# ScalarE writes the high halves of the projection phase, and two first-segment transposes use the score banks

## The chip, the cores and the metric

The kernel runs on one core of one Trainium2 chip. The metric is the device time of one execution in microseconds, median of the runs; lower is better.

## The reference

One transformer block over 2048 tokens of width 576, in fp32: adaptive layer norm, attention with 32 heads of width 18 in four segments of 512 tokens with a compressive memory carried from segment to segment, a residual, a second adaptive layer norm, a gated feed-forward layer of width 4608, and a second residual. Cut to what matters:

```python
mod = (silu(c) @ w_mod).reshape(1, 6, 1, 576)        # sa, ca, ga, sb, cb, gb
h = layernorm(x) * (1 + ca) + sa
q, k, v = h @ wq, h @ wk, h @ wv                      # 32 heads of 18, 4 segments of 512
for s in range(4):
    p = softmax(q_s @ k_s.T * scale + causal_mask)
    a_dot = p @ v_s
    a_mem = (phi(q_s) @ M) / (phi(q_s) @ z + 1e-6)    # phi(t) = t + 1 if t > 0 else exp(t)
    o_s = g * a_mem + (1 - g) * a_dot
    M, z = M + phi(k_s).T @ v_s, z + phi(k_s).sum()
x = x + ga * (concat(o) @ wo)
h = layernorm(x) * (1 + cb) + sb
x = x + gb * ((silu(h @ w_gate) * (h @ w_up)) @ w_down)
```

## The kernel before

Matrix products are made in a reduced fp32 format (F32R). To keep fp32 accuracy, an operand is split into a high part `hi` (the value rounded to F32R) and a low part `lo = x - hi`, and a product is made of three terms: high by high, low by high, high by low. Making a high part is one pass of an engine over the tile; making a low part is a subtraction on VectorE.

The kernel is one program without loops at run time. Python writes the instructions, and a planner then fixes the order of each engine's instructions from the order they were written in and from estimated durations; on the chip each engine works through its own list strictly in that order. The lists can therefore differ from the written order.

Three stages follow each other: the projection phase (the function's first part, pools opened at lines 244 to 251), the attention phase with the output projection, and the feed-forward layer. The change is in the projection phase only.

**Start.** TensorE multiplies the modulation weights `wm` with the conditioning vector into `pr` (line 356). ScalarE copies `pr` to `row` (lines 360 and 363), TensorE transposes it (`pcr`, line 367), and VectorE writes the per-feature scale and shift `colv` (lines 370 to 372). In the meantime VectorE normalises the first segment's four tiles of `x` in place (line 229).

**Transposed activations, `trans_in(s)`, line 408.** For each of five feature tiles `kt`, TensorE transposes the normalised `x` into a PSUM tile `pt` of tag `t`, which has two banks (line 234). `evac_split` (line 236) follows: ScalarE applies scale and shift from PSUM to an SBUF tile `f` (line 241, tag `hf`, two buffers), and `split` (line 78) makes the high part on GpSimd from `f` (line 79) and the low part on VectorE (line 80). The results are `hh[kt]` and `hl[kt]`, and for the last, half-filled tile `hr`, which holds both parts. They have one buffer each, so a segment's tiles can be written only when the value projection of the segment before has read the old ones.

**Query and key projection, `proj(s, t)`, line 456.** For each of nine output tiles, 14 matrix products accumulate in a bank `pp` (tag `p`, three banks; line 99). The bank is read once: ScalarE copies it to `f` (line 464), GpSimd makes `fh` from `f`, VectorE makes `fl`, and the queue of SyncE stores both to memory (lines 469 to 478). For key tiles `phi_k` (line 431) transposes `f` (`ptk`, line 435) and makes the feature map.

**Weights.** `split` is also used for the nine weight tiles `wqkh`/`wqkl` (line 294) and the five tiles `wvh`/`wvl` (line 511), each after its load (`wraw`, `wvraw`; four buffers).

**Other work of the phase.** `vproj` (line 483) makes the values (`pv`) and copies them out on ScalarE (line 496). `mem` (line 442) makes the memory matrices (`pm`), with a VectorE product (line 451) and a GpSimd sum (line 453). From segment 1 on, `early` begins the scores of the first two attention units: products in banks of tag `s1` (line 182), maxima on VectorE (line 187), a small GpSimd step (`mc`, `ml`, lines 192 to 195), a transpose `pmt` (line 201). The statistics of the next segment's layer norm use VectorE and one GpSimd power (`rs`, line 225). The eight PSUM banks are: two of tag `t`, three of `p`, one of `m`, two of `s1`.

Of the kernel before, what the change touches and what calls it, by code (L numbers as in the profile page):

```python
# [7 lines left out]
F32 = mybir.dt.float32  # L8
F32R = mybir.dt.float32r
BF16 = mybir.dt.bfloat16  # L10
AF = mybir.ActivationFunctionType
ALU = mybir.AluOpType
# [3 lines left out]
P = 128  # L16
# [6 lines left out]
L = 512  # L23
# [44 lines left out]
def f32(ap):  # L68
    return ap.bitcast(F32)
# [3 lines left out]
def block(ctx: ExitStack, tc: tile.TileContext, x, wqk, wv, wo, beta, wgu, wd, c, w_mod, out):  # L73
    nc = tc.nc
    def pool(stk, name, bufs=1, **kw):
        return stk.enter_context(tc.tile_pool(name=name, bufs=bufs, reuse_waits="tile", **kw))

    def split(hi, lo, src):
        nc.gpsimd.tensor_scalar(hi, src, 1.0, 0.0, op0=ALU.mult, op1=ALU.add)
        nc.vector.tensor_tensor(lo, src, f32(hi), op=ALU.subtract)  # L80

    def chain(*g):
# [133 lines left out]
    def ln_stats(wk, xs, n):  # L216
        st = wk.tile([P, n, 2, 6], F32, tag=f"st{n}", name="st")
        mv = wk.tile([P, n, 2], F32, tag=f"mv{n}", name="mv")
        rs = wk.tile([P, n], F32, tag=f"rs{n}", name="rs")
        for i in range(n):  # L220
            for h in range(2):
                nc.vector.bn_stats(st[:, i, h, :], xs[i][:, 288 * h:288 * h + 288])
            nc.vector.bn_aggr(mv[:, i, :], st[:, i, :, :])
        nc.vector.tensor_scalar(rs, mv[:, :, 1], EPS, None, op0=ALU.add)
        nc.gpsimd.tensor_tensor(rs, rs, mhalf[:, :n], op=ALU.pow)
        return mv, rs

    def xhat(dst, src, mv, rs, i):
        nc.vector.tensor_scalar(dst, src, mv[:, i, 0:1], rs[:, i:i + 1], op0=ALU.subtract, op1=ALU.mult)

    def transpose_group(pt, src, kt):
        for i in range(4):
            n = P if kt < 4 else 64
            nc.tensor.transpose(pt[:n, 128 * i:128 * i + 128], src(i)[:, 128 * kt:128 * kt + n], ident)

    def evac_split(wk, pt, kt, hi, lo, sc, bi, tag="hf"):
        f = wk.tile([P, L], F32, tag=tag, name="hf")
        n = P if kt < 4 else 64
        if kt == 4:
            hi, lo = hi[0:64], hi[64:128]  # L240
        nc.scalar.activation(f[:n], pt[:n], AF.Identity, scale=sc[:n], bias=bi[:n])
        split(hi, lo, f[:n])

    with ExitStack() as p1:
        wq1 = pool(p1, "wq1")
# [5 lines left out]
        ps = pool(p1, "ps1", 2, space=PSUM)  # L251
# [26 lines left out]
        def load_x(s):  # L278
            t = xs[s] = x1.tile([P, 4, D], F32, tag="x", name=f"x{s}")
            for i in range(4):  # L280
                r = L * s + P * i
                nc.sync.dma_start(t[:, i, :], x[r:r + P, :])
                yield
# [39 lines left out]
        with ExitStack() as p0:  # L323
            m0 = pool(p0, "m0")
            wm = {}
            gx = load_x(0)
            for p in (1, 0):
                for k in range(3):
                    wm[p, k] = m0.tile([96, 2, D], F32, tag=f"wm{p}{k}", name=f"wm{p}{k}")
                    nc.sync.dma_start(wm[p, k], wmv[p][:, 2 * k:2 * k + 2, :])  # L330
                    for _ in range(XP[3 * (1 - p) + k]):
                        next(gx)

            nc.scalar.activation(sg, cs, AF.Exp, scale=-1.0)
            nc.vector.tensor_scalar(sg, sg, 1.0, None, op0=ALU.add)
            nc.vector.reciprocal(sg, sg)
            nc.vector.tensor_tensor(sg, sg, cs, op=ALU.mult)

            nc.scalar.activation(gat, gat, AF.Exp, scale=-1.0)
            nc.vector.tensor_scalar(gat, gat, 1.0, None, op0=ALU.add)  # L340
            nc.vector.reciprocal(gat, gat)
            nc.vector.tensor_scalar(omg, gat, -1.0, 1.0, op0=ALU.mult, op1=ALU.add)

            for i in range(4):
                mv, rs = ln_stats(wk, [xs[0][:, i, :]], 1)
                xhat(xs[0][:, i, :], xs[0][:, i, :], mv, rs, 0)

            sgb = wk.tile([96, 6, 32], F32, tag="sgb", name="sgb", bufs=1)
            nc.vector.tensor_copy(sgb, sg.unsqueeze(2).to_broadcast([96, 6, 32]))
            pr = ps.tile([P, L], F32, tag="m", name="pr", bufs=1)  # L350
            for p in (1, 0):
                for k in range(6):
                    for h in range(2):
                        r = 64 * (1 - p) + 32 * h
                        w = wm[p, k // 2][:, k % 2, 256:576] if h else wm[p, k // 2][:, k % 2, 0:256]
                        nc.tensor.matmul(pr[r:r + 32, :320 if h else 256], lhsT=sgb[:, k, :], rhs=w,
                                         start=(k == 0), stop=(k == 5))
            row = wk.tile([P, L], F32, tag="hf", name="row")[:, :320]
            nc.gpsimd.memset(row[:, 256:], 0.0)
            nc.scalar.copy(row[:, :256], pr[:, :256])  # L360
            for p in (1, 0):
                r = 64 * (1 - p) + 32
                nc.scalar.copy(row[r:r + 32, 256:], pr[r:r + 32, 256:320])
            pc = ps.tile([P, 3, P], F32, tag="m", name="pcr", bufs=1)
            for b in range(3):
                n = P if b < 2 else 64
                nc.tensor.transpose(pc[:n, b, :], row[:, 128 * b:128 * b + n], ident)
            for p in (1, 0):
                c0 = 64 * (1 - p)
                nc.vector.tensor_scalar(colv[:, 0:2, 1 - p], pc[:, 0:2, c0], float(p), None, op0=ALU.add)  # L370
                nc.vector.tensor_scalar(colv[:, 2:4, 1 - p], pc[:, 0:2, c0 + 32], float(p), None, op0=ALU.add)
                nc.vector.tensor_scalar(colv[0:64, 4:5, 1 - p], pc[0:64, 2, c0 + 32:c0 + 33], float(p), None, op0=ALU.add)
# [35 lines left out]
        def trans_in(s):  # L408
            hh = [h1.tile([P, L], F32R, tag=f"hh{k}", name=f"hh{k}") for k in range(4)]
            hl = [h1.tile([P, L], F32R, tag=f"hl{k}", name=f"hl{k}") for k in range(4)]  # L410
            hr = h1.tile([P, L], F32R, tag="hr", name="hr")
            hT[s] = (hh, hl, hr)
            for kt in range(5):
                pt = ps.tile([P, L], F32, tag="t", name="pt")
                transpose_group(pt, lambda i: xs[s][:, i, :], kt)
                if kt < 4:
                    evac_split(wk, pt, kt, hh[kt], hl[kt], colv[:, kt, 0:1], colv[:, kt, 1:2])
                else:
                    evac_split(wk, pt, kt, hr, None, colv[:, kt, 0:1], colv[:, kt, 1:2])
                yield  # L420
# [35 lines left out]
        def proj(s, t):  # L456
            hh, hl, hr = hT[s]
            pp = ps.tile([P, L], F32, tag="p", name="pp", bufs=3)
            mm14(pp, lambda k: wqkh[:, t, k, :], lambda k: wqkl[:, t, k, :], lambda k: hh[k],
                 lambda k: hl[k], lambda: hr, True)  # L460
            f = pb.tile([P, L], F32, tag="pf", name="pf")
            fh = pb.tile([P, L], F32R, tag="fh", name="fh")
            fl = pb.tile([P, L], F32R, tag="fl", name="fl")
            nc.scalar.copy(f, pp)
            split(fh, fl, f)
            k0, k1 = 128 * t, min(128 * t + 128, D)
            if k0 < D:
                n = k1 - k0
                nc.sync.dma_start(kD[s][k0:k1, 0:2, :], f32(fh[:n]).unsqueeze(1).to_broadcast([n, 2, L]))
                nc.sync.dma_start(kD[s][k0:k1, 2, :], f32(fl[:n]))  # L470
            q0, q1 = max(128 * t - D, 0), 128 * t + 128 - D
            if q1 > 0:
                n = q1 - q0
                r = P - n
                nc.sync.dma_start(qD[s][q0:q1, 0:3:2, :], f32(fh[r:]).unsqueeze(1).to_broadcast([n, 2, L]))
                nc.sync.dma_start(qD[s][q0:q1, 1, :], f32(fl[r:]))
                if s > 0:
                    nc.sync.dma_start(qF[s][q0:q1, :], f[r:])
            return f
# [24 lines left out]
        for _ in trans_in(0):  # L504
            pass
# [8 lines left out]
        for s in range(NSEG):  # L514
# [12 lines left out]
            for t in QKORD:  # L527
# [4 lines left out]
                f = proj(s, t)  # L532
# [42 lines left out]
    ps = pool(p2, "ps2", 2, space=PSUM)  # L575
# [94 lines left out]
    op = pool(p2r, "op", side="right")  # L670
# [671 lines left out]
    with tc.manual_schedule():  # L1342
# [5 lines left out]
        for u in range(NU + 1):  # L1348
            s, q = divmod(u, 8)
# [22 lines left out]
        ps = pool(p2r, "pst", 2, space=PSUM)  # L1372
# [28 lines left out]
        for i in range(4):  # L1401
            for h in range(2):
                for c in range(WC):
                    n = 8 * i + 4 * h + c
# [28 lines left out]
        ps = pool(p4, "ps4", 1, space=PSUM)  # L1433
# [6 lines left out]
        n, nw = 0, PF  # L1440
# [5 lines left out]
        for t in range(2):  # L1446
            for p in range(NPR):
# [16 lines left out]
                for k in range(14):  # L1464
# [68 lines left out]
                    if prev is not None and is_plain(*prev):  # L1533
# [3 lines left out]
                        if CH0[t][k]:  # L1537
                            f = plain(*prev, chunk)
# [97 lines left out]
```

## Time and profile before

| what | value |
|---|---|
| median of 3 runs | 1909.57 us (1909.08 to 1915.14) |
| profiled execution: its time | 1911.3 us |
| profiled execution: span from first to last instruction | 1909.4 us |
| TensorE (PE) matmul busy | 1872.0 us, 98% |
| VectorE (DVE) busy | 1507.0 us, 79% |
| ScalarE (ACT) busy | 933.7 us, 49% |
| GpSimd (POOL) busy | 584.5 us, 31% |
| granted TensorE clock, mean | 0.998 |

How to read the views: times are microseconds from the first instruction. In the timeline a row gives start, duration, engine, line, operation, output and inputs, shape, count, and in square brackets how long the engine was idle before and what ended that. PE matmul rows overlap, since they are pipelined: the distance between starts says how fast they go. In the chain of waits each piece is the work or the wait that the next piece had to wait for. PEclk is the granted clock of TensorE, 1.00 being full. L79 is line 79.

### The profile page before, as it was taken

The page shows a single profiled execution, that of the slowest core. Times are in us where ns is not written, and L with a number is a line of the kernel's source. Part 1 is how long each engine was busy: PE and PEld are TensorE (multiplying, and loading weights), DVE is VectorE, ACT ScalarE, POOL GpSimd, SP SyncE. Part 2 cuts the span into 40 slices and gives each one's busy share as a digit, 9 for nine tenths or more (in the row PEclk, how much of TensorE's full clock was granted, in tenths as well). Part 3 has the DMA queues.
Part 4 walks back from the last instruction along what each step waited for, and adds up shares of the span by engine and source line. Part 5 has one row for each costly group of instructions (what it writes and reads, how often), then busy time and mean ns, then how long its engine had stood idle before and what let it go on. Part 6 is the DMA issues. An engine that isn't in the chain of part 4 may idle for free.

```text
span 1909.4 us, 30712 instructions
## 1 busy us (share of the span) xinstructions
PE 1872.0 (98%) x10927; PEld 1560.4 (82%) x10927; DVE 1507.0 (79%) x3273; ACT 933.7 (49%) x2060; POOL 584.5 (31%) x787
## 2 busy tenths in 40 slices
PE   7999999999999899999999999999999999999999
PEld 4888866676766788888888888888888888888888
DVE  6566358878886888888888888866888888888887
ACT  1222267768767543454454454444445454454542
POOL 5212236555556645435445435400000000000000
PEclk9999999999999999999999999999999999999999
DMA  6767555445654854454454554477333333333331
GB/s 199 258 220 255 197 177 152 132 138 155 195 157 129 311 199 154 161 196 143 162 192 141 183 164 129 153 263 231 102 124 102 95 105 101 123 102 101 108 105 59
DMA packets 179424, 304.31 MB, mean 159 GB/s; under 512 B 26152, under 2 KB 107688, under 8 KB 177352
## 3 DMA queue, kind: packets, MB, share of 16 engines
q1 hardware_dynamic: 150264, 244.40, 40.9%
q10 hardware_dynamic: 29008, 57.96, 8.6%
q8 instruction: 86, 1.41, 0.3%
q14 instruction: 66, 0.54, 0.1%
HBM read 187.98 MB, written 113.77 MB: 158 GB/s over the span
## 4 chain that ended last, share of the span: by engine, by line
PE 88%; DMA 3%; DVE 3%; ACT 2%; POOL 1%; issue 1%; SPq 1%; ACTq 0%; DVEq 0%; POOLq 0%
PE A L1202 23%; PE pd L1323 13%; PE C L1202 11%; PE pd L1306 9%; PE B L1202 6%; PE pp L99 5%; PE s L599 4%; PE av L619 3%; PE s L182 3%; PE pv L99 3%; PE pw L729 2%; DMA qs<-qD 1%; DMA y<-yD 1%; PE pn L800 1%; ACT Pt L602 1%
## 5 line engine op out<-in xcount | busy, mean ns | idle before, releaser
L1202 PE MATMUL A<-y,wh 128*128 128x512 f32 x1152 | 406.1, 393 | 3.4 <-ACT B L1248 1.0
L187 DVE CUSTOM_DVE_ANT_0 junk<-s,tri 128x256 bf16<-128x256 f32 (+3 forms) x512 | 228.8, 487 | 71.9 <-PE s L182 64.4
L1167 DVE TENSOR_TENSOR wl<-O,wh 128x256 fp32r<-128x256 f32 x504 | 260.3, 521 | 2.8 <-ACT wh L1166 2.3
L1202 PEld LDWEIGHTS A<-y,wh 128*128 128x128 f32 x1152 | 216.6, 188 | 47.6 <-ACT B L1248 1.5
L1202 PE MATMUL A<-y,wl 128*128 128x512 f32 x576 | 226.7, 394 | 0.0
L602 ACT ACTIVATE Pt<-s 128x512 f32<-128x512 f32 (+1 forms) x352 | 188.0, 559 | 75.2 <-PE s L599 70.9
L1157 POOL TENSOR_TENSOR O<-O 128x384 f32<-128x384 f32 x144 | 164.6, 1156 | 169.2 <-DMA O<-in_wgu_dram 65.0
L1311 DVE TENSOR_TENSOR acc<-acc,pd 128x576 f32<-128x576 f32 x216 | 162.4, 752 | 58.6 <-PE pd L1306 52.0
L1202 PE MATMUL C<-y,wh 128*128 128x512 f32 x576 | 202.6, 392 | 1.6 <-DVE cu L1225 1.6
L1166 ACT CAST wh<-O 128x256 fp32r<-128x256 f32 x504 | 196.9, 405 | 7.6 <-DVE wl L1167 3.5
L1323 PE MATMUL pd<-dh,al 128*128 128x288 f32 x640 | 189.1, 296 | 0.0
L1323 PE MATMUL pd<-dh,ah 128*128 128x288 f32 x640 | 189.1, 295 | 0.0
L1323 PE MATMUL pd<-dl,ah 128*128 128x288 f32 x640 | 188.9, 295 | 0.0
L1327 DVE TENSOR_TENSOR acc<-acc,pd 128x576 f32<-128x576 f32 x156 | 116.9, 750 | 90.4 <-PE pd L1323 90.0
L1266 ACT CAST ah<-sg 128x512 fp32r<-128x512 f32 x192 | 119.2, 621 | 84.0 <-DVE sg L1226 77.9
L599 PE MATMUL s<-qs,ks 110*128 110x512 f32 (+2 forms) x384 | 150.1, 407 | 2.1 <-ACT Pt L602 2.0
L182 PE MATMUL s<-ks,qs 108*128 108x256 f32 (+3 forms) x512 | 141.1, 328 | 5.9 <-DVE mx L187 3.6
L1267 DVE TENSOR_TENSOR al<-sg,ah 128x512 fp32r<-128x512 f32 x192 | 135.8, 707 | 8.8 <-ACT ah L1266 8.5
L1306 PE MATMUL pd<-dh,ah 128*128 128x288 f32 x448 | 133.0, 297 | 0.0
L1306 PE MATMUL pd<-dh,al 128*128 128x288 f32 x448 | 132.5, 296 | 0.0
L1306 PE MATMUL pd<-dl,ah 128*128 128x288 f32 x448 | 132.3, 295 | 0.0
L1202 PEld LDWEIGHTS C<-y,wh 128*128 128x128 f32 x576 | 108.3, 188 | 22.2 <-DVE cu L1225 2.1
(360 smaller groups left out, 4405.4 us busy)
## 6 DMA issues: line engine op xcount, KB each, us to landing
O<-in_wgu_dram SPq DMA_DIRECT2D x36, 768.0 KB
oD<-O ACTq DMA_DIRECT2D x36, 512.0 KB
O<-oD SPq DMA_DIRECT2D x36, 512.0 KB
ks<-kD SPq DMA_DIRECT2D x64, 216.0 KB
qs<-qD SPq DMA_DIRECT2D x64, 216.0 KB
O<-in_wgu_dram SPq DMA_DIRECT2D x36, 384.0 KB
rD<-wr ACTq DMA_DIRECT2D x36, 336.0 KB
wr<-rD SPq DMA_DIRECT2D x35, 336.0 KB
```

What stands on the lines that cost most here:

```text
L99: nc.tensor.matmul(ps, lhsT=a, rhs=b, start=(k == 0), stop=(k == 13))
L182: nc.tensor.matmul(bank[:, n * (h - h0):n * (h - h0) + n], lhsT=qst[b][0:108, h, 128 * i:128 * i + 128], rhs=kst[b][0:108, h // 2, 0:n], s ...
L187: nc.vector.tensor_tensor_reduce(junk[:, :n], bank[:, n * (h - h0):n * (h - h0) + n], tri[:, L - n:], 1.0, -3e38, op0=ALU.add, op1=ALU.max ...
L599: nc.tensor.matmul(bank[:, n * (g - h):n * (g - h + w)].rearrange("p (a b) -> p a b", a=w), lhsT=kst[u % NB][0:110, g // 2, 128 * j:128 * ...
L602: nc.scalar.activation(pt[:, h:h + per, :n], bank[:, :n * per].rearrange("p (a b) -> p a b", a=per), AF.Exp, scale=SCALE)
L1157: nc.gpsimd.tensor_tensor(o[:, d], o[:, a], o[:, b], op=op)
L1166: nc.scalar.copy(wh, o)
L1167: later.append(lambda: nc.vector.tensor_tensor(wl, o, f32(wh), op=ALU.subtract))
L1202: nc.tensor.matmul(bank, lhsT=a, rhs=b, start=(first and n == 0), stop=(n == 6), skip_group_check=not first)
L1306: nc.tensor.matmul(pd[:, i, :288], lhsT=a[:, tk], rhs=w, start=(k == 0), stop=(k == 2))
L1311: nc.vector.tensor_tensor(o, o, pd[:, :, :288], op=ALU.add)
L1323: nc.tensor.matmul(pd[:, i, :288], lhsT=a[:, tk], rhs=w, start=(k == 0), stop=(k == 5))
```

## The change

It makes four edits, all in the projection phase. `split` takes its high part with a ScalarE copy in place of a GpSimd pass (this is left in use for the weight tiles). `evac_split` and `proj` no longer call `split`: ScalarE reads the PSUM bank twice, first writing the high part and then the fp32 copy, and VectorE subtracts as before. The two small copies from `pr` into `row` go from ScalarE to VectorE. And the transposes of feature tiles 2 and 3 of the first segment go into the two banks of tag `s1`, which nothing else uses until segment 1.

```diff
     def split(hi, lo, src):
-        nc.gpsimd.tensor_scalar(hi, src, 1.0, 0.0, op0=ALU.mult, op1=ALU.add)
+        nc.scalar.copy(hi, src)
         nc.vector.tensor_tensor(lo, src, f32(hi), op=ALU.subtract)
...
+        nc.scalar.activation(hi, pt[:n], AF.Identity, scale=sc[:n], bias=bi[:n])
         nc.scalar.activation(f[:n], pt[:n], AF.Identity, scale=sc[:n], bias=bi[:n])
-        split(hi, lo, f[:n])
+        nc.vector.tensor_tensor(lo, f[:n], f32(hi), op=ALU.subtract)
...
-                nc.scalar.copy(row[r:r + 32, 256:], pr[r:r + 32, 256:320])
+                nc.vector.tensor_copy(row[r:r + 32, 256:], pr[r:r + 32, 256:320])
...
-                pt = ps.tile([P, L], F32, tag="t", name="pt")
+                pt = ps.tile([P, L], F32, tag="s1" if s == 0 and kt in (2, 3) else "t", name="pt", bufs=2)
...
+            nc.scalar.copy(fh, pp)
             nc.scalar.copy(f, pp)
-            split(fh, fl, f)
+            nc.vector.tensor_tensor(fl, f, f32(fh), op=ALU.subtract)
```

## The prediction

> **What bounds the kernel now.** I read the engines' shares first, then the stages (busy time of each engine per stretch), then inside the first 256 us, where the change lies, the chain of waits and the timeline.
>
> ```profile
> PE 1872.0 (98%) x10927; PEld 1560.4 (82%) x10927; DVE 1507.0 (79%) x3273; ACT 933.7 (49%) x2060; POOL 584.5 (31%) x787
> ```
> ```profile
> core 0: us, PE busy (x) PEld busy (x) DVE busy (x) ACT busy (x) POOL busy (x), PEclk, DMA share, GB/s
> ...
> 26.00:29.50 3.50, 2.96 (x10) 2.31 (x11) 2.98 (x4) 1.57 (x3) 3.09 (x4) 0.51 0.57 179
> 29.50:33.00 3.50, 3.50 (x12) 2.61 (x11) 3.50 (x4) 0.99 (x2) 3.03 (x4) 0.51 0.33 102
> ...
> 23.00:40.00 17.00, 12.67 (x49) 8.91 (x47) 14.25 (x19) 5.15 (x9) 10.74 (x12) 0.80 0.36 112
> 40.00:256.00 216.00, 213.11 (x1251) 184.53 (x1249) 113.38 (x252) 54.78 (x103) 51.35 (x81) 1.00 0.69 236
> 256.00:1910.00 1654.00, 1632.20 (x9579) 1360.04 (x9578) 1368.45 (x2974) 872.06 (x1945) 508.94 (x659) 1.00 0.47 149
> ```
>
> TensorE is the bound: 98% of the span, and 213.11 of the 216 us from 40 to 256, the rest of the projection phase. So high parts that are made elsewhere gain only where TensorE waits for them. The one place where it plainly does is 23 to 40 us: 12.67 of 17 us busy, and at half clock (0.51) from 26 to 33.
>
> ```profile
> 18.01 5.69 PE pr L356 x22
> ...
> 23.72 0.37 ACT row L360
> ...
> 24.11 0.20 ACT row L363
> ...
> 24.32 0.21 ACT row L363
> ...
> 25.55 0.79 ACT hf L241
> ...
> 26.41 1.20 POOL hh L79
> ...
> 37.06 1.04 DVE hr L80
> ...
> 38.15 1.90 PE pp L99 x7
> ...
> 40.48 3.26 PE pp L99 x14
> 43.74 0.44 PE ptk L435 x4
> ```
>
> This is the chain from the end of the modulation product to the steady state: ScalarE, GpSimd and VectorE hand each feature tile on, the last low part (`hr`) ends at 38.10, and from 38.15 everything is TensorE. One projection then costs 3.26 + 0.44 = 3.70 us, 3.26 / 14 = 0.23 per product, and the third one ends at 43.74.
>
> **Start: the sum.**
>
> ```profile
> 25.55 1.45 ACT L241 ACTIVATE hf<-pt,colv 128x512 f32<-128x512 f32 x2 [1.02 <-DVE colv L370]
> ...
> 28.25 1.05 PE L234 MATMUL pt<-ident,x 128*128 128x128 f32 x4
> ...
> 30.38 0.63 PE L99 MATMUL pp<-hh,wqkh 128*128 128x512 f32 x1
> ...
> 30.81 0.63 PE L99 MATMUL pp<-hh,wqkl 128*128 128x512 f32 x1
> ...
> 90.23 0.68 DVE L80 TENSOR_TENSOR hr<-hf,hr 64x512 fp32r<-64x512 f32 x1 [0.51 <-POOL hr L79]
> ```
> ```profile
> L1166 ACT CAST wh<-O 128x256 fp32r<-128x256 f32 x504 | 196.9, 405 | 7.6 <-DVE wl L1167 3.5
> ...
> L1266 ACT CAST ah<-sg 128x512 fp32r<-128x512 f32 x192 | 119.2, 621 | 84.0 <-DVE sg L1226 77.9
> ```
>
> Two activations back to back took 1.45 us, 0.79 for the first and 0.66 for the next. The changed chain has ten (high part and copy of five tiles), all on ScalarE: 0.79 + 9 x 0.66 = 6.7 us. One 640-column weight tile probably falls among them; no row shows a ScalarE pass over it, and the straight line through the casts (256 columns 0.405, 512 columns 0.621) gives 0.73; were it not there, the chain would be that much shorter, and with all three early weight tiles in it 1.5 longer. The two small row copies (0.20 and 0.21) on VectorE save between nothing, if they follow one another as now, and 0.4, if they hide behind the 0.37 copy; I count 0.2. The activations thus start at 25.4, the last ends at 32.8, and the subtraction, 0.68 undisturbed against 1.04 here, ends at about 33.6: 4.5 us before 38.10.
>
> "PSUM — Partial Sum Buffer" of the Trainium skill (section "PSUM bank collisions raise a hardware error") says that two engines must not use one bank in the same partitions at once, so the copies of `row` would have to follow one another. By it their move to VectorE gains nothing and the sum would be 0.2 smaller; no row here shows such a pair.
>
> TensorE cannot use all of the 4.5. From 30.38 to 30.81 is 0.43 per product at half clock, against 0.23 at full clock. With tiles 2 and 3 transposed ahead, which their two extra banks allow, it has before it four transposes (1.05 at half clock) and the 42 products of three projections. It starts on the first high part at 25.4 + 0.8 = 26.2. If half clock lasts to 33.0 as now, 6.8 - 1.05 = 5.75 us make 13 products; 29 at 0.23 take 6.7, the 0.44 of one `ptk` follows: the third projection ends at 40.1 against 43.74, 3.6 us earlier. The high end: full clock from 29.5, 5.3 us (worked out below, as a rival). The low end: the planner sets the eight extra transposes between the `pr` products, on the path at half clock, and delays the start by 2 x 1.05 = 2.1, leaving 1.5. I take **3.5**, near the first, since TensorE stands free from 23.7 on for such work.
>
> **The steady projections.**
>
> ```profile
> L79 POOL TENSOR_SCALAR fh<-pf 128x512 fp32r<-128x512 f32 x36 | 24.0, 668 | 80.3 <-ACT pf L464 66.4 <-issue 4.9 <-DVE pk L439 4.7
> ...
> L79 POOL TENSOR_SCALAR wvh<-wvraw 128x576 fp32r<-128x576 f32 x5 | 5.1, 1016 | 2.5 <-DMA wvraw<-in_wv_dram 2.5
> ```
> ```profile
> L464 ACT COPY pf<-pp 128x512 f32<-128x512 f32 x36 | 21.1, 586 | 66.2 <-PE pp L99 59.9 <-DMA qF<-pf 5.4 <-POOL rs L225 0.8
> ...
> L241 ACT ACTIVATE hf<-pt,colv 128x512 f32<-128x512 f32 x16 | 12.3, 777 | 20.3 <-DVE hl L80 17.5 <-PE pt L234 1.3 <-DVE colv L370 1.0
> L438 ACT ACTIVATE pe<-pe 128x512 f32<-128x512 f32 x12 | 7.6, 633 | 24.2 <-DVE pe L437 24.2
> ```
>
> ScalarE gains 36 x 0.586 = 21.1 us for `fh`, 16 x 0.777 = 12.4 for `hh`, four half tiles at about the same (3.1), and 14 weight tiles at 0.7 (9.8): 46 us in all. Of these some 38 fall after 40 us, so that it is busy for about 93 of the 216. The tightest stretch is segment 0, where one projection brings two copies (1.17), one exponential (0.63), one `wqkh` (0.73) and for a while one `wvh` (0.7): 3.2 of 3.70 us. It fits. The bank is held 0.6 us longer, but there are three of them, so TensorE has 2 x 3.70 us before it wants it back; `f` comes 0.6 later, but its transposes stand behind the next 3.26 us of products. I cost this at nothing. If that cover went, each of 36 projections would lose up to 0.6.
>
> **Waits that GpSimd's list makes now.**
>
> ```profile
> 101.63 0.44 PE L182 MATMUL s<-ks,qs 108*128 108x384 f32 x1 [0.97 <-DVE mx L187]
> ```
> ```profile
> 111.77 0.28 PE L201 MATMUL pmt<-ident,mc 128*32 128x128 f32 x1 [0.93 <-POOL mc L195]
> ```
> ```profile
> 109.53 0.08 DVE L187 DVE_READ_ACCUMULATOR2_ANT mx<- 128x1 f32 x1
> ```
> ```profile
> 110.00 0.62 POOL L79 TENSOR_SCALAR fh<-pf 128x512 fp32r<-128x512 f32 x1 [4.01 <-ACT pf L464]
> 110.58 0.21 POOL L192 TENSOR_SCALAR mc<-mx 128x16 fp32r<-128x16 f32 x1
> ```
>
> The maxima are through at 109.6, but at 110 the step `mc` stands behind `fh`, which waited for ScalarE. Without `fh` it starts about 0.9 earlier, and TensorE's 0.93 goes. The wait at 101.63 is VectorE's own list, and may stay: 0 to 0.97, I take 0.4. Together **1.3**.
>
> **Segment borders.**
>
> ```profile
> 142.53 0.30 PE L99 MATMUL pv<-wvl,hr 128*128 128x288 f32 x1
> ...
> 148.40 1.20 POOL L79 TENSOR_SCALAR hh<-hf 128x512 fp32r<-128x512 f32 x2
> ...
> 151.02 1.30 PE L448 MATMUL pm<-vs,pk 128*128 128x152 f32 x8 [0.23 <-DVE mbd L451]
> ...
> 153.32 0.40 PE L99 MATMUL pp<-hl,wqkh 128*128 128x512 f32 x1
> ...
> 153.99 0.50 PE L99 MATMUL pp<-hr,wqkh 128*128 128x512 f32 x1 [0.27 <-DVE hr L80]
> ```
>
> At the border of segments 1 and 2 the last `pv` is through at 142.8, the next high parts stand on GpSimd behind sums of `mem` until 148.40, and TensorE ends up waiting for `hr`: 0.67 between starts where 0.23 is normal, so 0.44, and 0.23 ahead of 151.02. On ScalarE the four tiles after the first need 0.79 + 7 x 0.66 = 5.4 us from about 143.3, and the subtraction 0.7: ready near 150, with over 3 us to spare. So the gain is 0.7 at this border. No row is shown for the next, which has the same work; I take as much for it, and nothing for the first: **1.4**, with 0 and 2 as ends. What is late next is TensorE itself.
>
> **The sum.** 3.5 + 1.3 + 1.4 = 6.2. Against it stand waits that a fuller, strictly ordered ScalarE brings: behind an activation that waits for a bank stand the copies of `pp` and `pv`, and behind a weight copy that waits for its load stand both. GpSimd waits 2.5 us for `wvraw` loads in all today, the bound if none were covered; below, nothing. I take 0.7, since the three banks cover each. Net 5.5: the profiled execution, 1911.3 us with a span of 1909.4, would become 1905.8. It stands 1.7 above the median of the runs shown, so the median goes from 1909.57 to **1904.0**. The forecast's own range is a gain of 2 to 8: low with the start at 1.5 and VectorE's and the weights' waits left, high with every term at its best.
>
> **Rivals.** The first is the clock. PEclk is 0.51 from 26 to 33, although TensorE is busy for 2.96 of 3.50 us in the first of the two stretches. If the earlier start fills that stretch, full clock may come at 29.5: 3.3 - 1.05 = 2.25 us make 5 products, the other 37 take 8.5 at 0.23, and with 0.44 the third projection ends at 38.4, 5.3 earlier. That is 1.8 more than I took: 1902.2. Against it, the stretch was nearly full already and that was not enough. "TensorE: Matmul & The Clock Gate" of the Trainium skill (Part 1) says that the clock opens after one sustained busy window of about 3.4 us. By that page this rival hangs on whether 26 to 29.5 is filled; the trace agrees with the length, the clock being full again two such stretches after 26. Chance 0.13.
>
> The second: the gain is swallowed.
>
> ```profile
> 270.90 4.68 DMA qs<-qD
> ```
>
> Behind the projections the chain passes a load of 4.68 us. If the start of the attention phase is set by such loads, an earlier start only waits longer there: 1909, no change. Against it, that load itself is issued behind work that moves with the rest. Chance 0.13.
>
> The third ends slower. The lists are planned, not written: transposes at 28.25 stand amid products of the projection. Changed durations may reorder the attention phase too, so that stacks are loaded later than their units need them. Each such wait costs about 4.68 us on the chain; two more (9.4 - 5.5 = 3.9 slower) are still within 0.3%, from three on it decides: 14.0 - 5.5 = 8.5, 1918. For it: 1654 us of kernel lie behind the change. Against: nothing there is written differently. Chance 0.11.
>
> **The numbers.** The forecast has 0.63. A measurement of this kernel can tell about 0.3% from no change, 5.7 us, and the forecast's 5.5 lies just inside: half of its chance (0.31) is faster by over 0.3%, half (0.32) within. The clock rival is faster (0.13), the swallowed gain the same (0.13), the replanned lists slower (0.11): 0.44, 0.45, 0.11. The range runs from 1899.5 (10 us gained: the clock, and every term at its best) to 1911 (nothing gained and a little lost), leaving out the slower case and thin tails.
>
> **What would show it.** Right: the run of full projections starts near 35, not 38.15; `hr` has no GpSimd ahead of it; ScalarE is busy for about 93 us from 40 to 256 where it had 54.78, and GpSimd for less than 20 where it had 51.35; the wait before `pmt` is gone; the last `pv` of segment 3 ends 5 to 6 us earlier, and the 1654 us behind keep their length. Wrong: TensorE waiting for ScalarE at the borders or in segment 0's projections, `pr` ending two or more us after 23.7, or a stretch after 256 that changes its length by more than about 2 us.

## The result and the profile after

The changed kernel takes 1903.98 us (median of 8 runs, 1901.1 to 1909.91), the kernel before 1913.22 (8 runs beside them, 1909.08 to 1918.15). The ratio is 0.9955, 95% interval 0.9944 to 0.9966: faster by 0.45%, or 8.6 us (the two medians lie 9.2 us apart). The forecast was 1904.0 and a gain of 5.5, counted from a median before of 1909.57 with three runs; with eight runs that median is 1913.22. So the gain was 3 us larger than forecast, and that the time was met to within 0.1 us is luck. The profiled execution took 1901.1 us with a span of 1899.4.

Busy shares, and the stretches of the first 256 us and the rest (columns: TensorE, weight loads, VectorE, ScalarE, GpSimd, each with its count; granted clock; DMA share; GB/s):

```profile
PE 1866.3 (98%) x10927; PEld 1559.4 (82%) x10927; DVE 1497.0 (79%) x3275; ACT 972.1 (51%) x2128; POOL 535.8 (28%) x717
```
```profile
26.00:29.50 3.50, 3.50 (x12) 2.85 (x11) 1.67 (x4) 3.50 (x7) 0.00 (x0) 0.61 0.94 318
29.50:33.00 3.50, 3.50 (x16) 2.81 (x16) 3.34 (x6) 3.05 (x5) 0.00 (x0) 1.00 0.80 249
...
23.00:40.00 17.00, 15.90 (x67) 12.67 (x68) 13.71 (x27) 14.74 (x24) 0.00 (x0) 0.90 0.70 239
40.00:256.00 216.00, 213.60 (x1267) 183.50 (x1266) 111.47 (x277) 89.73 (x168) 18.49 (x34) 1.00 0.70 236
```

From 23 to 40 us TensorE is now busy for 15.90 of 17 us where it was for 12.67, and GpSimd has nothing there. From 40 to 256, ScalarE took over much as forecast (89.73, forecast about 93), and GpSimd has 18.49 left. The chain of waits through the start, after:

```profile
11.35 2.35 PE pr L357 x8
...
15.42 1.20 PE pr L357 x8
...
21.31 0.37 ACT row L361
...
23.27 0.79 ACT hh L241
...
24.10 1.63 PE pp L99 x5
...
37.13 3.27 PE pp L99 x14
```

and two rows of the same view of the kernel before that the prediction doesn't show:

```profile
14.68 2.28 PE pr L356 x8
...
44.18 3.26 PE pp L99 x14
```

The chain no longer hops between three engines: behind the first activation it is TensorE almost throughout. The fourth projection starts at 37.13 where it started at 44.18, 7.05 us earlier. Two parts make this up: the activations start 2.28 earlier (23.27, was 25.55), because the `pr` products came to full pace earlier (eight took 1.20 where they took 2.28); and from there to the fourth projection it is 13.86 us where it was 18.63.

The timeline bounds the rest of the phase, by the first and the last value product; first before, then after:

```profile
65.05 0.29 PE L99 MATMUL pv<-wvh,hh 128*128 128x288 f32 x1
...
254.83 0.29 PE L99 MATMUL pv<-wvl,hr 128*128 128x288 f32 x1
```
```profile
58.01 0.30 PE L99 MATMUL pv<-wvh,hh 128*128 128x288 f32 x1
...
244.77 0.29 PE L99 MATMUL pv<-wvl,hr 128*128 128x288 f32 x1
```

Between them lie 190.1 us before and 187.1 after, so that 3.0 us come from segments 1 to 3 and their borders. From the last `pv` to the end it is 1654.3 us in both: nothing behind the phase changed its length. So the profile's 10.0 us are 7.0 at the start and 3.0 in the segments. TensorE's waits from 40 to 256, by the table of waits, before and after (total us, times, longest):

```profile
PE s L182 <- DVE mx L187: 1.0, 1, 1.0
PE pmt L201 <- POOL mc L195: 0.9, 1, 0.9
PE pp L99 <- DVE hr L80: 0.5, 2, 0.3
PE pm L448 <- DVE mbd L451: 0.5, 2, 0.2
```
```profile
PE s L601 <- ACT Pt L604: 1.1, 2, 0.6
PE pmt L201 <- POOL mc L195: 1.0, 2, 0.7
PE s L182 <- DVE mx L187: 0.2, 1, 0.2
```

The first row after is from the attention phase, which now begins before 256. The two border waits, on `hr` and on `mbd`, are gone. The wait on `mx` shrank. The wait of `pmt` did not go.

### The profile page after: what moved, and what is told of

Read it like the earlier page. It is cut to its first block, busy times and chain, and to the rows that moved or that the text cites. A ratio compares the mean times of both kernels' runs of the same rounds, so it can differ in the third digit from the quotient of the medians.

```text
span 1899.4 us, 30695 instructions
## 1 busy us (share of the span) xinstructions
PE 1866.3 (98%) x10927; PEld 1559.4 (82%) x10927; DVE 1497.0 (79%) x3275; ACT 972.1 (51%) x2128; POOL 535.8 (28%) x717
## 4 chain that ended last, share of the span: by engine, by line
PE 91%; DVE 4%; DMA 2%; ACT 1%; issue 1%; SPq 1%; POOL 0%; ACTq 0%; DVEq 0%
PE A L1204 24%; PE pd L1325 13%; PE C L1204 12%; PE pd L1308 9%; PE B L1204 6%; PE pp L99 6%; PE s L601 4%; PE av L621 4%; PE s L182 3%; PE pv L99 3%; PE pw L731 2%; DMA qs<-qD 2%; PE pm L449 1%; PE pn L802 1%; DVE junk L187 1%
```

## The experiments

Each kernel was run beside the kernel before on the same chip; ratios are to that. Single executions of one kernel spread by up to 10 us (before: 1907.93 to 1918.12 in 17 runs), so differences of 2 us between the times of single executions are not read as effects. Stretches inside the projection phase repeat more closely, as far as the clock is the same: from the first to the last value product the change took 187.1 us in both of its profiles. The theories that the expectations name: **A**, the hand-over of the feature tiles was long, and ScalarE alone makes it shorter. **B**, the two transposes in the score banks open the start. **C**, GpSimd's passes slow VectorE's subtractions, and taking them away is the gain. **D**, the clock opens earlier.

**One edit left out, or one alone.** The first kernel is the change without the transposes in the score banks; the second is the kernel before with those alone.

```diff
 no_s1, against the change
-pt = ps.tile([P, L], F32, tag="s1" if s == 0 and kt in (2, 3) else "t", name="pt", bufs=2)
+pt = ps.tile([P, L], F32, tag="t", name="pt")
 only_s1, against the kernel before
-pt = ps.tile([P, L], F32, tag="t", name="pt")
+pt = ps.tile([P, L], F32, tag="s1" if s == 0 and kt in (2, 3) else "t", name="pt", bufs=2)
```

> The changed kernel with all first-segment transposes back in the two banks of tag t. Theory A (the chain through ScalarE is shorter, and the transposes ahead only take work out of the half-clock stretch): the start loses 1 to 2 us of its 7, the rest stays; ratio to before near 0.9965, first full projection (the fourth) starts at 38 to 39 where before has 44.18 and the change 37.13. Theory B (the transposes ahead are what opens the start): nearly all of the 7 us is lost; ratio near 0.9985, the fourth projection at 42 to 44.

> The kernel before with only the transposes of tiles 2 and 3 in the score banks. Theory A: GpSimd and VectorE still hand the tiles on one by one, so 0 to 1 us; ratio 0.9995 to 1.0005, fourth projection near 43 to 44. Theory B: 3 us or more; ratio 0.998 or less, fourth projection near 40. If the earlier opening of TensorE's clock (15.1 where before has 22.7) comes from the added transposes and not from chance, pr ends near 21.5 here too, not at 23.7.

Without the transposes all of the gain stays: 0.9950 (0.9935 to 0.9964). Alone they are worth 0.17%: 0.9983 (0.9975 to 0.9992). The chain of waits of only_s1:

```profile
23.16 0.79 ACT hf L241
...
42.31 3.26 PE pp L99 x14
```

The activations start as early as in the change, but the hand-over through GpSimd then takes 19.15 us to the fourth projection, as long as before (18.63), and that starts only 1.87 earlier. B as the main cause falls.

The next two put ScalarE's high part into `evac_split` alone, and into `proj` alone.

```diff
 only_evac, against the kernel before (evac_split)
+nc.scalar.activation(hi, pt[:n], AF.Identity, scale=sc[:n], bias=bi[:n])
 nc.scalar.activation(f[:n], pt[:n], AF.Identity, scale=sc[:n], bias=bi[:n])
-split(hi, lo, f[:n])
+nc.vector.tensor_tensor(lo, f[:n], f32(hi), op=ALU.subtract)
 only_proj, against the kernel before (proj)
+nc.scalar.copy(fh, pp)
 nc.scalar.copy(f, pp)
-split(fh, fl, f)
+nc.vector.tensor_tensor(fl, f, f32(fh), op=ALU.subtract)
```

> The kernel before with only the segment tiles' high parts made by ScalarE from PSUM (evac_split); weights and query/key high parts stay on GpSimd. Theory A: the start gains 3 to 4 us and each of the two later borders about 1; the wait before the pmt transpose stays; ratio near 0.997. Theory C (VectorE's subtractions are slow because GpSimd's passes run beside them, 1.20 where 0.69 is undisturbed, and the gain is the end of that): GpSimd still makes the weight tiles, the start gains 1 us at most; ratio near 0.9985.

> The kernel before with only the query/key high parts made by ScalarE from PSUM (proj). Theory A: nothing at the start and the borders, about 1 us where GpSimd's step mc stood behind fh (TensorE's wait before the pmt transpose, 0.93, goes); ratio 0.9993 to 0.9997. Theory C: also faster VectorE work in segment 0; ratio near 0.999.

`evac_split` alone measured 0.9955 (0.9940 to 0.9969), the same as the whole change; `proj` alone 0.9994 (0.9982 to 1.0005), which can't be told from nothing. Lines of their tables of waits, first of only_evac, which has no row of `pp` or `pm`, then the border waits of only_proj:

```profile
PE pmt L201 <- POOL mc L195: 0.5, 1, 0.5
```
```profile
PE pp L99 <- DVE hr L80: 0.5, 2, 0.3
PE pm L448 <- DVE mbd L451: 0.5, 2, 0.2
```

It is `evac_split` that takes the border waits away; they stay where only `proj` is changed. From the first to the last value product only_evac has 187.0 us and only_proj 188.9, against 190.1: the 3.0 us of the segments are there with `evac_split` alone. What only_proj does take away is the wait of `pmt`: its table has no such row up to 250 us. Its gain lies in segment 1, which takes 61.03 us from the last value product of segment 0 to its own, where it took 62.25. The chain of waits of only_evac:

```profile
25.07 0.79 ACT hh L241
...
39.65 3.26 PE pp L99 x14
```

From the first activation to the fourth projection it is 14.58 us where it was 18.63, with the start itself moved by only 0.48. (The profiled execution of only_evac, 1907.31 us, is the slowest of its five, whose median is 1903.97; what is longer in it lies behind the last value product, 1658.0 us.)

Both together, without the other edits:

```diff
 evac_proj: only_evac and only_proj in one kernel
```

> The kernel before with the high parts of the activations alone (evac_split and proj) made by ScalarE from PSUM; weights, row copies and transposes as before. Theory A: these two carry the change; borders gain 1 us each, the wait before pmt goes, the start gains 4 to 6; ratio to before 0.995 to 0.9957, the last pv of segment 3 ends near 246.5 to 247.5 (before 255.1, the change 245.1). Theory C (the weight tiles on GpSimd slow VectorE): ratio 0.997 or more, the last pv near 250.

0.9954 (0.9939 to 0.9969); from the first to the last value product 187.1 us. `proj` adds nothing that can be measured to `evac_split`.

**What moving the weights does.** One kernel puts the weight tiles' high parts back on GpSimd; the other moves only them to ScalarE.

```diff
 weights_pool, against the change (split)
-nc.scalar.copy(hi, src)
+nc.gpsimd.tensor_scalar(hi, src, 1.0, 0.0, op0=ALU.mult, op1=ALU.add)
 only_weights, against the kernel before (split; evac_split and proj keep their GpSimd pass, written out)
-nc.gpsimd.tensor_scalar(hi, src, 1.0, 0.0, op0=ALU.mult, op1=ALU.add)
+nc.scalar.copy(hi, src)
```

> The change with only the weight tiles' high parts given back to GpSimd. Theory A: nothing to 1 us either way: the 640-column pass (0.66) leaves ScalarE's chain, some VectorE subtractions beside GpSimd take 1.2 in place of 0.69; ratio to before 0.995 to 0.956 of the change's range, that is 0.9950 to 0.9960; last pv at 244.5 to 246. Theory C: the start loses 2 us or more, last pv at 247 or later, ratio 0.9967.

> The kernel before with only the weight tiles' high parts moved from GpSimd to ScalarE. Theory C: VectorE's subtractions in the start fall from 1.20 to about 0.7 and hr ends 2 to 4 us before 38.1; ratio 0.998 to 0.999. Theory A: the hand-over from ScalarE to GpSimd to VectorE stays, at most 1 us is gained; ratio 0.9995 to 1.0005.

weights_pool measured 0.9942 (0.9924 to 0.9960), not to be told from the change; only_weights 0.9978 (0.9969 to 0.9986). The groups of `hl` from 20 to 40 us (minimum/median/maximum ns, first and last start), in the kernel before, in only_evac, in only_weights and after:

```profile
L80 DVE TENSOR_TENSOR hl<-hf,hh x4: 1094/1203/1207, 27.6 to 33.2; 128x512 fp32r<-128x512 f32 x4
```
```profile
L243 DVE TENSOR_TENSOR hl<-hf,hh x4: 683/688/1199, 26.6 to 31.9; 128x512 fp32r<-128x512 f32 x4
```
```profile
L243 DVE TENSOR_TENSOR hl<-hf,hh x4: 679/891/1092, 24.0 to 29.5; 128x512 fp32r<-128x512 f32 x4
```
```profile
L243 DVE TENSOR_TENSOR hl<-hf,hh x4: 676/694/694, 25.5 to 29.4; 128x512 fp32r<-128x512 f32 x4
```

The same subtraction takes 1.20 us where GpSimd works all the time and 0.69 where it has nothing, and only_weights gains at least what was expected for C (0.998 to 0.999). So C's mechanism is real, but C as the whole cause falls: with the weights back on GpSimd, the gain stays. A as the whole cause falls with only_weights, where the tiles' high parts remain on GpSimd and the time is still 0.22% shorter. In that kernel the activations start at 22.50 and the fourth projection at 37.82, 15.32 us, against 18.63 before and 14.58 in only_evac: either of the two loads taken off GpSimd ends most of the delay, and the other one then has little left to take. (Half clock lasted 3.4 us in these two and 6.8 before, which is a part of the difference; the next section sets this apart.) What only `evac_split` does is the borders: from the first to the last value product only_weights has 190.3 us, as before.

**The clock.** The change once more, for the scatter of the start:

```diff
 after_again: the change, unaltered
```

> The change once more, beside the next two. Theory D: the clock's windows run freely, so the opening may shift by up to 3.4 us, but it stays before 18; pr ends at 21 to 22.3, last pv at 244.5 to 247; ratio to before 0.9944 to 0.9966.

0.9951 (0.9937 to 0.9964). Its chain of waits, and the two stretches in which it had half clock; then the only such stretch up to 256 us of the change's first profile:

```profile
15.75 2.28 PE pr L357 x8
...
24.67 0.79 ACT hh L241
...
39.69 3.28 PE pp L99 x14
```
```profile
24.83:28.25 3.42, 2.75 (x8) 2.04 (x9) 2.88 (x5) 3.42 (x6) 0.00 (x0) 0.50 0.47 133
28.25:31.66 3.41, 3.41 (x11) 2.70 (x10) 1.94 (x3) 3.41 (x6) 0.00 (x0) 0.50 0.82 260
```
```profile
25.35:28.76 3.41, 3.41 (x12) 2.77 (x11) 2.21 (x4) 3.41 (x6) 0.00 (x0) 0.50 0.90 304
```

The same program has its fourth projection 2.56 us later than in its first profile: the second eight `pr` products still ran at half pace, and half clock, gone by 28.76 there, lasts until 31.66 here. By the trace's records of the granted clock every half-clock stretch of this part, in all profiles, is 3.41 us long or twice that. In the first profile TensorE filled the stretch (3.41 us busy), and full clock followed; here it came to its products later and was busy for 2.75 of 3.42, half clock stayed for another 3.41 us, which were filled, and then went. In the kernel before it is the same: 2.96 of 3.41 us kept half clock, the next 3.41 were full and ended it at 32.91. Taken in pieces of 3.41 us, each piece at half clock with 3.2 us or more of work was the last of its stretch; of the five with 2.7 to 3.1 one was (only_evac, 2.84). From the first to the last value product it has 187.1 us, as the first profile. So the 3.0 of the segments are steady, and the start is 7.0 in one profile and 4.5 in the other.

Ten unused products of 128 x 128 (each is two instructions in the trace), five behind `pr` and five behind `pcr`, fill TensorE's gap at the end of the modulation product; here in the kernel before, in the change, and in weights_pool:

```diff
 before_fill, after_fill and pool_fill: against the kernel before, the change and weights_pool
+wu = ps.tile([P, L], F32, tag="p", name="wu", bufs=3)
+for i in range(5):
+    nc.tensor.matmul(wu[:, :P], lhsT=wm[0, 2][:, 1, 448:576], rhs=ones[0:96, :], start=True, stop=True)
 row = wk.tile([P, L], F32, tag="hf", name="row")[:, :320]
...
+for i in range(5):
+    nc.tensor.matmul(wu[:, :P], lhsT=row[:, :P], rhs=ones, start=True, stop=True)
 for p in (1, 0):
     c0 = 64 * (1 - p)
```

> The kernel before plus the same ten products. Theory A: the clock is full from 26 on, but hr still ends near 38 because ScalarE, GpSimd and VectorE hand the tiles on one by one; fourth projection at 43 to 44.2 where before has 44.18; ratio 0.9993 to 1.0003. Theory D alone (the clock carries the start's gain): fourth projection at 41 or earlier, ratio 0.9985 or less.

> The change plus ten small 128x128 products whose result nobody reads: five after the pr products, five after the pcr transposes, where TensorE stands idle. Theory D (the clock falls to half at 25.3 because the stretch before it is mostly idle): the half-clock stretch of 3.4 us is gone, the first pv starts near 56.5 to 57.3 where the change has 58.0, last pv near 244; ratio to before about 0.9948. Rival: the clock falls anyway or the products delay pcr; first pv at 58 to 58.5.

> The change with the weights' high parts back on GpSimd and the ten unused products in TensorE's idle gaps around pcr. If both small gains are real, 1 us faster than the change: ratio to before 0.9940 to 0.9950, last pv at 243.5 to 245. Rival: they were only the clock's phase, and it equals the change within its interval.

In the kernel before they gain 0.21%: 0.9979 (0.9969 to 0.9989). Its chain and one of its stretches:

```profile
24.18 0.79 ACT hf L241
...
41.26 3.26 PE pp L99 x14
```
```profile
26.00:29.50 3.50, 2.87 (x14) 1.82 (x14) 3.24 (x3) 0.78 (x1) 3.02 (x5) 1.00 0.62 191
```

The clock is full where it was 0.51, and the fourth projection starts 2.92 earlier, 1.55 of it from the way behind the first activation (17.08 us, was 18.63); but the tiles still come by way of GpSimd, and TensorE is busy for only 2.87 of 3.50 us. So theory D has a share there: about half of what the whole change gives. With the change the products gain nothing beyond it: 0.9948 (0.9932 to 0.9965). On weights_pool they measured 0.9969 (0.9958 to 0.9981), no better than that kernel without them (0.9942, 0.9924 to 0.9960) and short of the 0.9940 to 0.9950 that was expected; the two intervals just touch, and as the last value product starts at 245.9 here and at 246.5 there, the profiles don't show where time was lost. In after_fill's profile the half clock is gone, and its chain reads:

```profile
11.99 2.35 PE pr L357 x8
...
24.02 0.79 ACT hh L241
...
37.20 3.26 PE pp L99 x14
```

From the first activation to the fourth projection it is 13.18 us where the change's first profile has 13.86, so that the half clock cost 0.7 at least. At full clock the next limit shows: TensorE waits 0.4 us for `hr`, whose subtraction stands on VectorE behind statistics (line 222) of a tile of `x` that landed at 31.66 only. The first modulation weights landed 0.64 later in this execution (11.99 against 11.35), and the fourth projection starts at 37.20 against 37.13. What is left to win by the clock in the change is less than the intervals can show.

The way from the first activation to the fourth projection can now be compared at like clock. With the tiles' and the weights' high parts on GpSimd it took 18.6 to 20.2 us where half clock lasted 6.8 us of it (before, only_proj, only_s1, before_early below) and 17.1 where there was none (before_fill). With `evac_split` on ScalarE it took 15.0 and 15.1 at 6.8 us of half clock (after_again, weights_pool), 13.9 to 14.7 at 3.4 (the change, only_evac, evac_proj) and 13.2 to 13.7 at none (no_s1, after_fill, pool_fill). So `evac_split` is worth some 3.5 us of this way at either clock, and 6.8 us of half clock mostly 1.5 to 2.

The last one tests whether the score banks' transposes help by keeping TensorE busy between the modulation weights' loads: eight unused products there instead, in the kernel before.

```diff
 before_early, against the kernel before
+wu = ps.tile([P, L], F32, tag="p", name="wu", bufs=3)
 for p in (1, 0):
     for k in range(6):
+        if p == 1 and k == 4 or p == 0 and k == 0:
+            for i in range(4):
+                nc.tensor.matmul(wu[:, :P], lhsT=wm[1, 1 if p else 2][:, 1, 448:576], rhs=ones[0:96, :],
+                                 start=True, stop=True)
         for h in range(2):
```

> The kernel before plus eight unused 128x128 products, four behind the second and four behind the third tile of modulation weights, in the place where the change has eight more transposes. Theory D (the clock opens because TensorE is kept busy there, whatever with): the clock opens at 18 or earlier where before has 22.7, pr ends 1 us or more before 23.7 in spite of the added work, ratio 0.998 to 0.9995. Rival (it was chance, or something about the transposes): opening at 19.9 to 23.5 as in every run without them, and pr ends 1 to 2 us later than 23.7; ratio 1.0 to 1.001.

It is slower: 1.0016 (1.0007 to 1.0025).

```profile
13.62 2.01 PE wu L356 x8
...
18.66 1.09 PE wu L356 x8
...
23.86 0.37 ACT row L365
...
45.86 3.27 PE pp L99 x14
```
```profile
40.00:44.00 4.00, 4.00 (x16) 3.27 (x15) 3.19 (x5) 1.22 (x2) 3.16 (x4) 0.71 0.80 282
```

The added 3.10 us were paid back by faster `pr` products and transposes, since `row` starts 0.14 later only. But in this profile half clock came back amid the projections (0.71 from 40 to 44), where before it was full, and the fourth projection starts 1.68 later.

No kernel here beat the change by more than the intervals: the best, weights_pool (0.9942), overlaps it.

## Why the prediction was right, and where its sizes were off

**Right: where the gain lies, and how much `evac_split` shortens the hand-over.** "ScalarE gains 36 x 0.586 = 21.1 us for `fh`, 16 x 0.777 = 12.4 for `hh`" came out as said: the groups after have

```profile
L465 ACT CAST fh<-pp 128x512 fp32r<-128x512 f32 x36 | 21.1, 586 | 54.6 <-PE pp L99 48.6 <-issue 3.7 <-DMA qD<-fh 2.2
L241 ACT ACTIVATE hh<-pt,colv 128x512 fp32r<-128x512 f32 x16 | 12.5, 782 | 10.4 <-PE pt L234 10.1 <-DVE colv L371 0.3
```

The ten activations with one weight tile among them were put at 7.4 us, and ScalarE's timeline has just that, 23.27 to 30.67, with one 640-column pass of 0.72 where 0.73 was taken from the line through the casts:

```profile
23.95 0.72 ACT L79 CAST wqkh<-wraw 128x640 fp32r<-128x640 f32 x1
...
29.88 0.79 ACT L242 ACTIVATE hf<-pt,colv 64x512 f32<-64x512 f32 x1
```

**Mis-sized: "I take 3.5".** The term of the start measured 7.0 in one profile and 4.5 in the other, and the last value product came 10.1 and 7.5 us earlier where 5 to 6 was said. The part that was worked out, from the first activation on, was 3.5 (the 3.6 less the 0.15 by which the start was put earlier). It measured 3.6 where the half clock lasted as long as before (after_again: 15.02 against 18.63) and 4.8 where it did not (13.86). What had no term is the modulation product itself. The prediction had the extra transposes between the `pr` products only as its low end, "on the path at half clock", with a delay of 2.1. They were put there (groups of 8, 6 and 2 in the chain), but TensorE reached full clock earlier with them: its clock record opens at 15.1 us in the change's first profile, at 22.7 before, at 15.1 to 18.0 in all six profiles with these transposes and at 19.9 to 23.5 in the others but for before_early (18.5) and only_weights (16.8). Counted back from the opening in pieces of 3.41 us, it came with them after the first piece in which TensorE was busy throughout; without them it took three such pieces in five profiles, two in before_fill and before_early, and one in only_weights. From the first `pr` product to `row` it is 9.96 us in the change's first profile (11.35 to 21.31) and 12.43 before (11.29 to 23.72). In the other five profiles with these transposes it is 9.9 to 11.3; in those without, the unused products of before_early left out, 11.9 to 12.7, but 11.3 in before_fill and 9.8 in only_weights. So the transposes shorten the modulation product mostly, not always; what in them opens the clock is not shown. That no_s1 is as fast without them has two reasons in its profile: no half clock behind the first activation, and 1.2 us less in its segments (185.9 from the first to the last value product). All of that is in segment 1, where its waits of `pmt` and on `mx` are 0.5 us against 1.2; why the rest, and whether its other executions are alike, is open.

**Nothing, where 0.2 was counted: the row copies.** They ran on VectorE behind ScalarE's copy, not beside it:

```profile
21.72 0.46 DVE L364 COPY row<-pr 32x64 f32<-32x64 f32 x2 [4.91 <-ACT row L361]
```

From the start of `row` to the first activation it is 1.96 us after and 1.83 before. "PSUM — Partial Sum Buffer" of the Trainium skill (section "PSUM bank collisions raise a hardware error") would have them follow one another, and they do: VectorE was released by ScalarE's copy. No run here shows what the two would do at once.

**Right in sum, wrong in place: the waits of GpSimd's list.** "Without `fh` it starts about 0.9 earlier, and TensorE's 0.93 goes" failed. After, the timeline reads

```profile
102.99 0.58 POOL L192 TENSOR_SCALAR mc<-mx 128x16 fp32r<-128x16 f32 x1 [11.73 <-DVE mx L187]
...
104.21 0.28 PE L201 MATMUL pmt<-ident,mc 128*32 128x128 f32 x1 [0.68 <-POOL mc L195]
```

GpSimd had been idle for 11.73 us; `mc` starts as soon as the maxima are through, as forecast. But TensorE arrives at `pmt` earlier too, `mc` takes 0.58 us where it took 0.21, and 1.0 us of waits remain there. With `proj` alone the step came out as said: `mc` takes 0.20, the wait is gone, and segment 1 is 1.2 shorter; it does not add to what `evac_split` gives. The wait on `mx` went from 1.0 to 0.2, twice the 0.4 that was allowed for it. From the last value product of a segment to that of the next, the kernel before has 62.25, 57.45 and 54.84 us and the change 61.35, 56.37 and 53.79. So segment 1, with these waits (put at 1.3) and the first border (put at nothing), gave 0.9, and the other two borders 1.1 each where 0.7 was counted: 3.0 against 2.7 in sum. only_evac has the same three lengths, so that `evac_split` alone gives all of it. The border rows read for the prediction, and the 1.0 us that the table of waits has for both borders together, held about half to two thirds of what went; where in the borders the rest lay was not followed.

**Not seen: 0.7 for ScalarE's ordered list.** TensorE has no wait on a ScalarE pass of the projection phase from 40 to 256, and evac_proj, with both second reads of PSUM, is as fast as only_evac. The bank held longer is hidden, as the prediction said.

**The rivals.** The clock rival came true in part, and by the way it named: full clock was back by 29.5 in the first profile, where TensorE filled the stretch before, and not in after_again, where it did not. "TensorE: Matmul & The Clock Gate" of the Trainium skill (Part 1) gives a window of about 3.4 us, and the trace agrees: half clock lasted 3.41 us, one window, in the first profile and 6.83, two, in after_again. Where these windows lie against the program differs from one execution to the next (the first ends at 28.76 or at 28.25), and no run here shows what sets it. The swallowed gain and the replanned lists are wrong: the 1654.3 us behind the phase kept their length within what executions scatter (1653.2 in after_again, 1652.9 to 1658.0 over all profiles). So the measured 8.6 lies between the sums of the two profiles, 4.5 + 3.0 and 7.0 + 3.0.

## What to carry to other kernels

Where a chain hands a tile from one engine to another and back, a second read of PSUM by the engine that already reads it can be cheaper than a pass of a third engine over the copy, as long as that engine has room: one such line in `evac_split` alone measured as much as the whole change. Two loads on a shared third engine can be substitutes, so price edits singly and together before adding their gains. An idle row does not measure what its cause costs, in either direction: here the two borders gave twice the time that the table of waits had for them, while the wait of `pmt` was put at 0.93 and stayed. And where the clock changes between executions, compare stretches that had it alike.

## What the runs showed of the hardware

**The clock moves the start by microseconds between executions of one program.** Eight `pr` products behind the change's first transposes took 1.20 us in one profile and 2.28 in the next, and the fourth projection differed by 2.56 us. Half clock came in pieces of 3.41 us, and one that TensorE filled with work was the last.

**The granted clock reads full before its first record.** In the kernel before:

```profile
14.00:17.00 3.00, 3.00 (x13) 1.23 (x12) 1.84 (x3) 0.00 (x0) 1.89 (x5) 1.00 1.04 251
```

The column shows 1.00 in this stretch, while eight of its `pr` products took 2.28 us, at half the pace of the 1.20 after; the first record of its clock is at 22.7 us. Early in a program the pace of equal products tells more than the column.

**GpSimd beside VectorE can nearly double a subtraction.** 128 x 512 takes 1.20 us while GpSimd makes high parts all the time and 0.69 where it does not. Not each one is hit: in only_evac one took 0.69 beside a GpSimd pass over 640 columns, and those passes took 1.13 to 1.25 us themselves, where 0.72 is the undisturbed time.

**Keeping TensorE busy early is not a gain by itself.** Eight unused products between the modulation loads left the end of `pr` where it was, and in the profile half clock came back later, in the projections: 1.0016.
